# A ring of six one-chunk input buffers, and weights spaced for it, in a kernel of linear attention and soft mixture of experts

The kernel runs on one core of one Trainium2 chip. The metric is the device time of one execution in microseconds (us). A run is called slow when it lies over 1.5% above the fastest of the same kernel; only fast runs are compared. Expectations and captions call the changed kernel "after" and the original "before".

## What must be computed

The first half is a linear attention with a decaying state (4 batches, 8 heads, 768 steps, head size 48), the second a soft mixture of 8 experts with 4 slots each over all 3072 tokens of width 384.

```python
for t in range(S):                       # attention; r, k, v are [4, 8, 768, 48] float32
    cur = einsum('bhd,bhe->bhde', u * k[t], v[t])
    y[t] = einsum('bhd,bhde->bhe', r[t], state + cur)
    state = w * state + einsum('bhd,bhe->bhde', k[t], v[t])
x = y as [3072, 384]
logits = x @ phi                         # [3072, 32]
slots = softmax(logits, over tokens).T @ x
slot_out[e] = relu(slots[e] @ w1[e]) @ w2[e]   # w1 [8, 384, 1024], w2 [8, 1024, 384] float32
out = softmax(logits, over slots) @ slot_out   # [3072, 384]
```

No up-projection can start before the attention of all tokens is done, because the first softmax is over tokens.

## The kernel before

The attention works in 12 chunks of 256 steps, three to a batch. A chunk has 384 KB each of r, k and v. In SBUF one partition holds two neighbouring steps of a head, so a contiguous piece of a chunk, at both ends, is 2 x 48 floats, 384 bytes. Input copies are issued by SyncE and land in a pool of two batch-sized buffers. The first batch is loaded chunk by chunk, the other three with one copy for each of k, r and v.

```python
ld = ctx.enter_context(tc.tile_pool(name="ld", bufs=2))
SRC = ((1, k), (0, r), (2, v))

def load_part(bt, i):                    # first batch only: one chunk, 384 KB a copy
    for x, src in SRC:
        nc.sync.dma_start(out=bt[:, x, :, i, :],
                          in_=src[0, :, i * TS:(i + 1) * TS, :].rearrange("h (p j) d -> p h (j d)", j=J))

def load(b):                             # batches 1 to 3: three chunks, 1.18 MB a copy
    if b >= B:
        return
    bt = new_batch(b)
    for x, src in SRC:
        nc.sync.dma_start(out=bt[:, x].rearrange("p h i m -> p (h i) m"),
                          in_=src[b].rearrange("h (i p j) d -> p (h i) (j d)", p=P, j=J))
# ... cut ...
            if n % nSb == 1:             # in the loop over chunks: batch b+2 after chunk 1 of batch b
                load(n // nSb + 2)
```

GpSimd (POOL) issues the weights, which are cast from float32 to bf16 on the way, in between the three products it makes for each chunk. So a stalled product also delays the weights behind it.

```python
def w1_load(e):
    nc.gpsimd.dma_start(out=w1_all[:, e, :, :], in_=w1_ap[:, e, :, :])
# w_todo: w1 of experts 0 to 7, then w2 of experts 0 to 6, then w2 of expert 7 in four pieces
# experts 4 to 7 of w2 ("w_tail") lie in a batch buffer that has come free
W_IN = [0, 0, 1, 0, 0, 1, 1, 1, 1]       # weights issued inside mults(n + 3), by chunk n
W_AT = [0, 0, 1, 0, 0, 1, 1, 1, 3, 0, 0] # weights issued at the end of iteration n
# ... cut: load_w(2) before the loop ...

def mults(n, inner=0):                   # cut to chunks 1 to 11
    nc.gpsimd.tensor_mul(rr[:, :, :, 0:D], r_l, W_n[:])
    load_w(inner)
    nc.gpsimd.tensor_mul(kk[:, :, :, 0:D], k_l, W_k[:])
    nc.gpsimd.tensor_mul(ku, ku, u_b)
```

The rest of the attention takes from there: VectorE's `rkv` product (L283) needs POOL's last product, ScalarE's `v_bf` copy needs v. Then come the up-projection (`h_p`), two down-projections (`so_p`, `sr_p`), a scaled copy `so_r`, and the output.

The softmax here doesn't subtract the row's maximum and nothing guards it: scores larger than these inputs give would overflow.

## Time and profile before

| | before |
|---|---|
| median of the first 3 runs | 128.2 us (128.12 to 129.5) |
| span of the profiled execution | 126.4 us |
| up-projection starts on PE | 96.92 us |
| `so_r` starts | 108.83 us |
| moved by DMA in all | 31.78 MB |

Queue q0 holds what POOL issues, q1 what SyncE issues; the columns are packets, MB and share of the 16 engines' time.

```profile
DMA packets 23080, 31.78 MB, mean 251 GB/s; under 512 B 10451, under 2 KB 18005, under 8 KB 23061
...
q0 software_dynamic: 5360, 15.19, 56.7%
q1 hardware_dynamic: 17280, 16.32, 41.8%
```

The 36 chunk-sized pieces of input (3 tensors, 12 chunks) have 1024 rows of 384 bytes each, 36,864 rows in all. Yet q1 counts only 17,280 packets, and the output is among them. The nine copies of the first batch are 9 x 1024 = 9216 packets of 384 bytes; they make up most of the 10,451 "under 512 B". The other 18,005 - 10,451 = 7554 under 2 KB are mostly the nine batch-sized copies: each goes in 768 packets of 1536 bytes, four rows to a packet. The stretch from 15.91 to 20.50 us, in which only such copies moved, shows it directly: 983 packets, 1.48 MB, so 1506 bytes each.

### The profile page before, as it was taken

What the parts mean: (1) busy time and instruction counts of PE and PEld (TensorE: products, weight loads), DVE (VectorE), ACT (ScalarE), POOL (GpSimd) and SP (SyncE); (2) the same over time, 40 slices, a digit from 0 to 9 for tenths busy, and PEclk for the clock granted to TensorE, in tenths of its full rate; (3) what the DMA queues carried; (4) which work ended last, traced back from release to release, by engine and by line L of the source; (5) the groups of instructions that cost most, each with busy time, mean ns of one, the idle gap of its engine ahead of it and who ended that gap; (6) DMA issues with size and microseconds to landing.
All of it is one profiled execution on the core that took longest, in us unless ns stands there. A gap on an engine that the chain in (4) does not pass through costs nothing.

```text
span 126.4 us, 4165 instructions
## 1 busy us (share of the span) xinstructions
PE 97.5 (77%) x1783; PEld 70.5 (56%) x1783; DVE 91.7 (73%) x181; ACT 78.4 (62%) x144; POOL 81.4 (64%) x77
## 2 busy tenths in 40 slices
PE   3994898887599969189798969799999998793000
PEld 3493575665487757177576657677665565520000
DVE  5599989969989999578999798979762411497000
ACT  5869498868479968488597688886431510495000
POOL 6009999799999799999999999992420000055100
PEclk9999999999959999977999599958999999995555
DMA  3999998999999999999999999999999998079992
GB/s 84 299 325 325 335 327 264 321 208 251 265 332 267 235 259 270 340 289 270 258 255 252 226 211 223 221 214 215 210 218 212 218 199 160 2 264 372 381 403 81
DMA packets 23080, 31.78 MB, mean 251 GB/s; under 512 B 10451, under 2 KB 18005, under 8 KB 23061
## 3 DMA queue, kind: packets, MB, share of 16 engines
q0 software_dynamic: 5360, 15.19, 56.7%
q1 hardware_dynamic: 17280, 16.32, 41.8%
q8 instruction: 14, 0.23, 0.7%
q10 hardware_dynamic: 420, 0.00, 0.2%
q14 instruction: 6, 0.04, 0.1%
HBM read 39.38 MB, written 4.72 MB: 349 GB/s over the span
## 4 chain that ended last, share of the span: by engine, by line
POOL 33%; DMA 25%; PE 10%; SPq 9%; DVE 8%; issue 4%; ACT 2%; POOLq 1%; DVEq 0%
DMA w_tail<-in_moe_w_dram 16%; POOL kk L256 10%; POOL rkv L257 9%; DMA rkv<-in_r_dram 8%; SPq L75 7%; POOL rr L254 7%; DVE o_s L748 5%; POOL w_all L187 2%; POOL w_h L194 2%; PE t_p L312 2%; POOL hT L121 1%; SPq L83 1%; PE so_p L681 1%; PE sr_p L712 1%; PE aat_p L331 1%
## 5 line engine op out<-in xcount | busy, mean ns | idle before, releaser
L343 DVE TENSOR_TENSOR at_s<-aat_p,mask 128x512 bf16<-128x512 f32 x47 | 30.2, 684 | 4.0 <-PE aat_p L331 3.8
L254 POOL TENSOR_TENSOR rr<-rkv,W_n 128x768 bf16<-128x768 f32 x11 | 19.9, 1813 | 8.9 <-DMA rkv<-in_r_dram 8.7
L257 POOL TENSOR_TENSOR rkv<-rkv,u_rep 128x768 f32<-128x768 f32 x11 | 19.9, 1812 | 0.9
L256 POOL TENSOR_TENSOR kk<-rkv,W_k 128x768 bf16<-128x768 f32 x11 | 20.0, 1817 | 0.1
L331 PE MATMUL aat_p<-t_rr,t_kk 64*64 64x128 bf16 x376 | 12.1, 243 | 7.8 <-ACT t_kk L319 4.7
L277 ACT COPY rpun<-rkv 128x384 f32<-128x384 f32 x23 | 11.3, 490 | 10.3 <-PE rpun L491 8.2
L331 PEld LDWEIGHTS <-t_kk 64*64 64x64 bf16 x384 | 8.6, 119 | 11.2 <-ACT t_kk L319 6.9
L283 DVE TENSOR_TENSOR rkv<-rkv,rpun 128x384 f32<-128x384 f32 x23 | 12.6, 546 | 1.3 <-POOL rkv L257 1.1
L301 DVE TENSOR_TENSOR dv<-v_bf,rpun 128x768 bf16<-128x768 bf16 x12 | 11.4, 953 | 2.4 <-ACT v_bf L264 1.4
L319 ACT COPY t_kk<-t_p 128x1024 bf16<-128x1024 bf16 x12 | 12.2, 1014 | 1.0 <-PE t_p L312 1.0
L752 POOL DMA_DIRECT2D out_dram<-o_s x1 | 0.6, 552 | 18.4 <-ACT o_s L750 18.4
L294 DVE TENSOR_REDUCE rpun<-rkv 128x16 f32<-128x768 f32 x12 | 11.5, 961 | 0.4
L382 PE MATMUL s_p<-v_bf,kk 64*128 64x96 bf16 x160 | 11.8, 222 | 0.0
L319 ACT COPY t_rr<-t_p 128x1024 bf16<-128x1024 bf16 x11 | 11.2, 1016 | 0.5 <-PE t_p L312 0.3
L391 DVE TENSOR_TENSOR st<-s_p,wm 128x384 bf16<-128x384 f32 x20 | 10.9, 546 | 0.4 <-PE s_p L382 0.4
L264 ACT CAST v_bf<-rkv 128x768 bf16<-128x768 f32 x12 | 10.0, 830 | 1.8 <-DMA rkv<-in_v_dram 1.8
L382 PEld LDWEIGHTS <-kk 64*128 64x128 bf16 x160 | 8.5, 104 | 4.0 <-issue 3.9
L433 ACT COPY xt_s<-xl_p 128x768 bf16<-128x768 bf16 x11 | 8.8, 798 | 1.4 <-PE xl_p L431 1.1
L412 ACT CAST x_t<-y_p 128x384 bf16<-128x384 f32 x22 | 9.6, 495 | 0.0
L488 PE MATMUL rpun<-Lexp,x_t 128*128 128x32 bf16 x66 | 5.1, 179 | 5.2 <-DVE dv L301 5.2
L312 PE MATMUL t_p<-ident,kk 128*128 128x128 bf16 x96 | 8.8, 246 | 0.2 <-ACT t_rr L319 0.2
L312 PE MATMUL t_p<-ident,rr 128*128 128x128 bf16 x88 | 8.5, 253 | 0.0
(132 smaller groups left out, 194.7 us busy)
## 6 DMA issues: line engine op xcount, KB each, us to landing
w_all<-in_moe_w_dram POOLq DMA_DIRECT2D x8, 768.0 KB, 11.6
w_h<-in_moe_w_dram POOLq DMA_DIRECT2D x4, 768.0 KB, 13.2
w_tail<-in_moe_w_dram POOLq DMA_DIRECT2D x3, 768.0 KB, 19.7
out_dram<-o_s POOLq DMA_DIRECT2D x6, 384.0 KB, 6.7
out_dram<-o_s SPq DMA_DIRECT2D x5, 384.0 KB, 6.1
rkv<-in_k_dram SPq DMA_DIRECT2D x3, 384.0 KB, 4.4
rkv<-in_r_dram SPq DMA_DIRECT2D x3, 384.0 KB, 4.6
rkv<-in_v_dram SPq DMA_DIRECT2D x3, 384.0 KB, 5.3
```

What stands on the lines that cost most here:

```text
L254: nc.gpsimd.tensor_mul(rr[:, :, :, 0:D], r_l, W_n[:])
L256: nc.gpsimd.tensor_mul(kk[:, :, :, 0:D], k_l, W_k[:])
L257: nc.gpsimd.tensor_mul(ku, ku, u_b)
L277: nc.scalar.copy(rp, loads[n][0][:, j, :, :])
L283: nc.vector.tensor_mul(s["ku"][:, j, :, :], s["ku"][:, j, :, :], s["rps"][j])
L294: nc.vector.tensor_reduce(d, s["ku"], axis=mybir.AxisListType.X, op=ALU.add)
L301: nc.vector.tensor_mul(dv[:], s["v"][:], d[:, :, :, None].to_broadcast([P, J, H, D]))
L312: nc.tensor.transpose(t_p[:, q, :, j, :], s[nm][:, j, 2 * q:2 * q + 2, :].rearrange("p h d -> p (h d)"), ident[:])
L319: nc.scalar.copy(t_s[:], s.pop("p_" + nm)[:])
L331: nc.tensor.matmul(at_p[a][g * HF:(g + 1) * HF, q, :], kT[sl, q, g, j, :], rT[sl, q, g, :, :].rearrange("p j c -> p (j c)"), start=True, s ...
L343: nc.vector.tensor_mul(s["at"][:, a, j, :, :], at_p[a][:], mask[:, j, None, :].to_broadcast([P, nP, P]))
L382: nc.tensor.matmul(s_p[:, q * D2:(q + 1) * D2], s["kk"][sl, j, 2 * q:2 * q + 2, :].rearrange("p h d -> p (h d)"), s["v"][sl, j, 2 * q:2 * ...
```

## The change

The intent is a finer ring: a chunk's buffer comes free as soon as that chunk is done, so loads need not wait for a whole batch, and r comes first, because POOL's first product wants it. The bytes in SBUF are the same. The weights are spaced differently to leave room for the inputs. Experts 4 to 7 of w2 take one pair of chunk buffers each. SyncE sends both halves of the first output. The core of the diff:

```diff
-    ld = ctx.enter_context(tc.tile_pool(name="ld", bufs=2))
+    ld = ctx.enter_context(tc.tile_pool(name="ld", bufs=6))
-            nc.sync.dma_start(out=bt[:, x].rearrange("p h i m -> p (h i) m"),
-                              in_=src[b].rearrange("h (i p j) d -> p (h i) (j d)", p=P, j=J))
+        b, i = divmod(n, nSb)
+        bt = ld.tile([P, 3, H, J * D], f32, name="rkv")
+        for x, src in SRC if n == 0 else (SRC[1], SRC[0], SRC[2]):
+            nc.sync.dma_start(out=bt[:, x],
+                              in_=src[b, :, i * TS:(i + 1) * TS, :].rearrange("h (p j) d -> p h (j d)", j=J))
 ... load(0) .. load(5) at the start, then in the loop:
-            if n % nSb == 1:
-                load(n // nSb + 2)
+            load(n + 1 + NL)
 ... weights
-        W_IN = [0, 0, 1, 0, 0, 1, 1, 1, 1]
-        W_AT = [0, 0, 1, 0, 0, 1, 1, 1, 3, 0, 0]
+        W_IN = [0, 0, 1, 0, 1, 1, 1, 1, 1]
+        W_AT = [0, 0, 0, 0, 1, 1, 1, 1, 2, 0, 0]
-        load_w(2)
+        load_w(1)
 ... last expert of w2 in pieces of 4, 2, 2 columns instead of 2, 2, 2, 2; output
-            put = nc.sync.dma_start if i % 2 == 0 else nc.gpsimd.dma_start
+            put = nc.gpsimd.dma_start if i and i % 2 == 0 else nc.sync.dma_start
-                    (nc.sync if j == 0 else nc.gpsimd).dma_start(out=out_ap[i][:, j, :], in_=o_s[:, j, :])
+                    put(out=out_ap[i][:, j, :], in_=o_s[:, j, :])
```

More of the change, by code (lines that the diff above doesn't have):

```diff
@@ L57, with load @@
     w1_all = wts.tile([P, E, nM, F], bf, name="w1_all")
-    w2_h = [wts.tile([P, E // 2, nF, Dm], bf, name="w2_h")[:]]
+    w2_h = wts.tile([P, E // 2, nF, Dm], bf, name="w2_h")
+    w2_of = [w2_h[:, e] for e in range(E // 2)]
     ident = wts.tile([P, P], bf, name="ident")
-    ld = ctx.enter_context(tc.tile_pool(name="ld", bufs=2))
+    ld = ctx.enter_context(tc.tile_pool(name="ld", bufs=6))
     cst = ctx.enter_context(tc.tile_pool(name="cst", bufs=1))
     loads = {}
+    NL = 6
     SRC = ((1, k), (0, r), (2, v))
-    def new_batch(b):
-        bt = ld.tile([P, 3, H, nSb, J * D], f32, name="rkv")
-        for i in range(nSb):
-            loads[b * nSb + i] = [bt[:, x, :, i, :].rearrange("p h (j d) -> p j h d", j=J) for x in range(3)]
-        return bt
-    def load_part(bt, i):
-        for x, src in SRC:
-            nc.sync.dma_start(out=bt[:, x, :, i, :],
-                              in_=src[0, :, i * TS:(i + 1) * TS, :].rearrange("h (p j) d -> p h (j d)", j=J))
-    def load(b):
-        if b >= B:
-            return
-        bt = new_batch(b)
-        for x, src in SRC:
-            nc.sync.dma_start(out=bt[:, x].rearrange("p h i m -> p (h i) m"),
-                              in_=src[b].rearrange("h (i p j) d -> p (h i) (j d)", p=P, j=J))
-    b_first = new_batch(0)
-    load_part(b_first, 0)
+    def load(n):
+        if n >= nS:
+            return
+        b, i = divmod(n, nSb)
+        bt = ld.tile([P, 3, H, J * D], f32, name="rkv")
+        loads[n] = [bt[:, x].rearrange("p h (j d) -> p j h d", j=J) for x in range(3)]
+        for x, src in SRC if n == 0 else (SRC[1], SRC[0], SRC[2]):
+            nc.sync.dma_start(out=bt[:, x],
+                              in_=src[b, :, i * TS:(i + 1) * TS, :].rearrange("h (p j) d -> p h (j d)", j=J))
+    load(0)
     warm = cst.tile([P, 1], f32, name="warm")
@@ L101 @@
                             in_=w.rearrange("(q a) d -> a d q", a=2)[par])
-    for i in range(1, nSb):
-        load_part(b_first, i)
-    load(1)
+    for n in range(1, NL):
+        load(n)
     row_i = cst.tile([P, 1], mybir.dt.int32, name="row_i")
@@ L189, in w2_load @@
     def w2_load(e, f0=0, f1=nF):
-        if e == XE and f0 == 0:
-            tail = ld.tile([P, (E - XE) * nF * Dm], bf, name="w2_tail", tag="rkv",
-                           padded_shape=[P, 3 * H * nSb * 2 * J * D])
-            w2_h.append(tail[:].rearrange("p (e f d) -> p e f d", e=E - XE, f=nF))
-        nc.gpsimd.dma_start(out=w2_h[e // XE][:, e % XE, f0:f1, :], in_=w2_ap[:, e, f0:f1, :])
+        if e >= XE and f0 == 0:
+            tail = ld.tile([P, nF * Dm], bf, name="w2_tail", tag="rkv", padded_shape=[P, 2 * 3 * H * J * D])
+            w2_of.append(tail[:].rearrange("p (f d) -> p f d", f=nF))
+        nc.gpsimd.dma_start(out=w2_of[e][:, f0:f1, :], in_=w2_ap[:, e, f0:f1, :])
     w_todo = []
@@ L199 @@
     w_todo.pop()
-    for f in range(0, nF, 2):
-        w_todo.append((w2_load, (E - 1, f, f + 2)))
+    for f0, f1 in ((0, 4), (4, 6), (6, nF)):
+        w_todo.append((w2_load, (E - 1, f0, f1)))
     w_todo.reverse()
@@ L535 @@
         v_cast(0)
+        load(NL)
         tables()
@@ L681, in down @@
                     nc.tensor.matmul(so_p[c * ES:(c + 1) * ES, :], hT[:, x, fi, c * ES:(c + 1) * ES],
-                                     w2_h[x][:, c, fi, :],
+                                     w2_of[x * XE + c][:, fi, :],
                                      start=(x == 0 and fi == 0), stop=(x == 1 and fi == nF - 1),
@@ L712, in last_down @@
                     nc.tensor.matmul(sr_p[c][:], hL[:, fi, :, :].rearrange("p g t -> p (g t)"),
-                                     w2_h[1][:, XL, fi, c * HD:(c + 1) * HD],
+                                     w2_of[E - 1][:, fi, c * HD:(c + 1) * HD],
                                      start=(fi == 0), stop=(fi == nF - 1), skip_group_check=True)
-        last_down(0, 2)
         keep(2)
-        last_down(2, 4)
+        last_down(0, 4)
         keep(1)
```

## The prediction

> **What bounds the kernel now.** I read first the busy row by slices on the profile page, then the chain of work that ended last, then the waits, and last the engine-by-stretch table (us, then PE, PEld, DVE, ACT and POOL busy, clock, DMA share, GB/s).
>
> ```profile
> DVE  5599989969989999578999798979762411497000
> DMA  3999998999999999999999999999999998079992
> GB/s 84 299 325 325 335 327 264 321 208 251 265 332 267 235 259 270 340 289 270 258 255 252 226 211 223 221 214 215 210 218 212 218 199 160 2 264 372 381 403 81
> ```
>
> Two engines look full: VectorE until some 93 us, and the DMA engines from 3 to 107 us and again from 111 to 124. The GB/s row has two levels while the DMA row stays at 9: about 330 early (r, k, v, plain float32 copies) and about 214 later (weights, cast from float32 to bf16, so twice as much is read as is counted).
>
> ```profile
> 84.04 20.84 DMA w_tail<-in_moe_w_dram
> 104.88 0.04 issue
> 104.93 1.46 PE so_p L681 x22
> 106.39 0.44 PE sr_p L712 x4
> ...
> 108.46 0.34 PE sr_p L712 x4
> 108.80 0.02 issue
> 108.83 0.43 ACT so_r L727
> ```
>
> This is the chain, in order of time. The second down-projection stands until expert 6 of w2 lands at 104.88, 20.84 us after its issue: with the queue full, that is a place in a line and not a slow transfer. From there PE runs without a gap to 108.80, then the normalisation and the output follow. So this landing sets the end, and POOL, which the chain names for a third of the span, matters only in so far as it issues late.
>
> ```profile
> POOL rr L254 <- DMA rkv<-in_r_dram: 8.7, 3, 6.8
> ACT v_bf L264 <- DMA rkv<-in_v_dram: 1.8, 1, 1.8
> DVE dv L301 <- ACT v_bf L264: 1.4, 1, 1.4
> DVE rkv L283 <- POOL rkv L257: 1.1, 1, 1.1
> PE so_p L681 <- DMA w_tail<-in_moe_w_dram: 0.5, 1, 0.5
> ```
>
> These are rows of the waits (total us, times, longest). The batch-sized loads do hurt the attention: POOL waits three times for r, and VectorE loses 1.4 us to a late v and 1.1 us to a late product of POOL. But the last line shows how little that side leads or trails: PE comes to the landing only 0.5 us early, after six filler products (L689) that took 1.15 us.
>
> ```profile
> 14.00:20.00 6.00, 6.00 (x109) 4.60 (x108) 5.47 (x10) 5.07 (x9) 5.92 (x4) 1.00 1.09 330
> 20.50:22.00 1.50, 1.11 (x25) 0.74 (x24) 1.46 (x3) 1.45 (x3) 1.50 (x3) 1.00 0.69 200
> 25.50:28.50 3.00, 2.70 (x51) 2.08 (x50) 1.91 (x4) 2.05 (x3) 2.92 (x3) 1.00 1.11 209
> 54.00:55.00 1.00, 0.88 (x24) 0.71 (x24) 0.65 (x3) 0.83 (x3) 1.00 (x2) 1.00 0.80 190
> 72.00:104.00 32.00, 29.58 (x576) 21.02 (x574) 22.26 (x42) 17.69 (x36) 16.16 (x22) 0.94 1.06 214
> 106.00:107.50 1.50, 1.50 (x19) 0.99 (x13) 0.56 (x1) 0.00 (x0) 0.00 (x0) 1.00 0.58 102
> ```
>
> Here the DMA share is the next to last number: above 1 in full stretches, 0.69 and 0.80 in the two stretches where the queues ran thin, 0.58 where the last weights trickle in.
>
> **A budget for the DMA.** Inputs: 3 tensors x 12 chunks x 384 KB = 14.16 MB. At 330 GB/s that is 42.9 us (the first batch, in chunk pieces, ran at 325 from 6.5 to 13.5 us, which adds 0.2). Weights: 16 x 768 KB = 12.58 MB written, at 214 GB/s 58.8 us. Together 101.9 us. The DMA begins at about 2.3 us and the weights trickle out by 107, so 104.7 us are used and 2.8 us lost. What I can point to: start-up from 2.5 to 6.5 us at 297, 0.4 us; 20.5 to 22 us, share 0.69 against 1.09, 0.55 us; 54 to 55 us, 0.25 us; the trickle, 0.7 us; the remaining 0.9 us is spread over the mixed stretches. Whatever the change does to waits of POOL or VectorE, it can bring the last landing forward only out of these 2.8 us.
>
> **What the Trainium skill says.** (1) "DMA: Bandwidth & Descriptors", Queues, rings and completion order: each DMA engine goes round the queues packet by packet. The trace agrees: from 25.5 to 28.5 us the total is 209 GB/s, the weights' own rate, although SyncE had issued k of the third batch at 24.89; large weight packets crowd small input packets out. Weights sent early delay inputs, which is what spacing is for. (2) "HBM Reference", Specifications (TRN2): a core streaming alone reaches about 425 GB/s, bounded by its 16 engines. The weights' 214 GB/s written is 428 read, so that stretch has no more to give. (3) The DMA page, Rules for kernel authors, advises at least 1 MiB per DMA. The change cuts loads of 1.1 MB to 384 KB. The trace shows no such penalty with copies back to back: 325 against 330 GB/s. (4) Its Specifications put the first byte at about 1 us for copies issued by GpSimd and 0.6 us for SyncE. The trace agrees in direction: the first two output halves landed 2.5 us after SyncE's issue and 3.5 us after GpSimd's.
>
> **The change part by part.**
> Chunk ring. Removed: the batch-grained release, where chunks 6 to 8 could not start before chunk 2 was done (issue at 24.89). Added: 36 SyncE issues in place of 18, about 1.15 us each by the rows of the first batch, 41 us on an engine with nothing else to do. Chunks 6 and 7 can follow at once behind chunk 5, because chunks 0 and 1 are used up by 12 and 19 us. So the hole at 20.5 us closes: 0.55 us. Each x of a chunk is now contiguous in a partition, so I expect the first batch's packets to become like those of the later ones: 0.2 us at most.
> Order r, k, v. r of chunk 1 is sent second-tensor-first instead of after k, one copy of 384 KB earlier: about 1.2 us at 325 GB/s. POOL's 6.8 us wait shrinks to about 5.6. VectorE is not waiting for it there (its row has no gap before its first product of chunk 1), so nothing of it reaches the end.
> Spaced weights. One weight instead of two after the second chunk, two by the fifth chunk instead of four. POOL's step per chunk is 3 x 1.81 = 5.43 us plus 0.6 to 0.8 us per weight issue, so it runs from about 8.5 us to about 76 us, 3 to 4 us ahead of now. I checked that the DMA stays fed. From 24 us the queue holds chunks 6 and 7 (3.6 us each) and one weight (3.7 us), work until about 35; chunks 8 to 11 come free some 6.5 us apart and weights from 33 us on, faster than they drain, so a backlog of 4 us or more remains. No new hole, and the one at 54 us closes: 0.25 us.
> Attention. The stalls of 1.4 and 1.1 us go, so attention and the up-projection finish about 2.5 us earlier. But the second down-projection then waits some 3 us for expert 6 instead of 0.5: the landing still decides.
> w2 tail. The four buffers are free long before their issue at 75 to 80 us (chunk 9 is done one iteration earlier), so no wait. Three pieces of expert 7 instead of four save one POOL issue, 0.53 us, beside a full DMA queue: nothing. The same products and fillers follow; the first piece is now needed whole, which may cost 0.1 us.
> First output. Both halves from SyncE. The second half was issued by POOL at 111.02, and from 111.5 to 112.0 the DMA ran at only 89 GB/s; filling part of that saves about 0.2 us. The rest of the output runs at 383 GB/s and is not touched.
> Sum: 0.55 + 0.25 + 0.2 (packets) + 0.2 (output) - 0.1 = 1.1 us. 128.2 - 1.1 = **127.1 us**.
>
> **Rivals.**
> A: the attention chain is the true bound, and the end follows it by the whole 2.5 us, perhaps with an earlier first chunk: about 125.5. For it: PE arrives only 0.5 us before the landing. Against it: a 20.84 us landing and a full DMA row; weights cannot land faster than they are read.
> B: the spacing starves the DMA. If POOL falls behind, or SyncE stands on a ring buffer while few weights are queued, holes of 1 to 2 us appear between 30 and 60 us: about 129. For it: only two weights are queued by the fifth chunk. Against: the backlog worked out above.
> C: small input packets now compete with weights through the whole attention and arrive late, so VectorE's stalls move rather than go. The DMA total stays the same: about 128.
> D: mixing at chunk grain recovers the 0.9 us of unexplained loss as well: about 126.2.
>
> **Range and chances.** The middle is the budget; D and half of A give the low side, B and C the high side. Range 125.8 to 128.5. Over 2% faster means below 125.6, which needs nearly the whole 2.8 us; chance 0.14. Slower by over 2% means above 130.8, which needs a large new hole: 0.03. Within 2%: 0.83.
>
> **What would show it right or wrong.** Right: DMA at 9 without the hole at 20 us; POOL's total wait for r under 6.5 us; the waits of VectorE for v_bf and for POOL's product gone; attention ending some 2 to 3 us earlier; PE's wait for w_tail grown to 2 to 4 us; the last w_tail of 768 KB landing near 104; the first output near 109 us. Wrong: weights moving clearly faster than 214 GB/s, expert 6 landing before 102.5, or a DMA share under 0.9 in any stretch of 2 us between 6 and 104.

## The result

| | before | after |
|---|---|---|
| runs side by side | 128.12, 128.2, 129.5; slow: 132.33 | 135.55, 136.11; slow: 141.65, 151.54 |
| median of all four | 128.85 us | 138.88 us |
| ratio of fast runs, 95% interval | | 1.056 (1.045 to 1.068) |
| span of the profiled execution | 126.4 us | 134.3 us |
| up-projection starts | 96.92 us | 105.97 us |
| `so_r` starts | 108.83 us | 117.10 us |

A ratio here and below is the mean time of one kernel's fast runs over that of the other's fast runs of the same rounds, so it is not quite the ratio of the medians in the table. The kernel became 5.6% slower where 0.9% faster was expected.

The span grew by 7.9 us. By the three marks: the attention ends 105.97 - 96.92 = 9.05 us later; from there to `so_r` it takes 11.13 us instead of 11.91, 0.78 less; from `so_r` to the end 17.2 instead of 17.57, 0.37 less. So the whole loss lies in the attention, and the rest gave a little back.

POOL's and the DMA's busy rows by slices of 1/40 of the span (3.36 us), and the rate under them, after:

```profile
POOL 6049999999999999990840059999950000014100
DMA  3999999999999999999999999999999999049993
GB/s 89 303 325 325 325 293 236 201 286 246 245 205 295 255 245 215 238 215 207 211 212 214 225 259 267 218 230 214 215 212 212 221 206 180 10 164 349 379 397 124
```

The DMA engines are as full as before until the output. POOL is not: it stands around 62 us and from 68 to 79 us. The waits (us in all, times, longest) say for what:

```profile
POOL rr L244 <- DMA rkv<-in_r_dram: 15.7, 2, 10.1
...
DVE rkv L273 <- POOL rkv L247: 5.7, 2, 5.5
...
POOL kk L246 <- DMA rkv<-in_k_dram: 3.5, 1, 3.5
...
ACT v_bf L254 <- DMA rkv<-in_v_dram: 2.7, 1, 2.7
```

The 15.7 us are 5.6 for chunk 1, as predicted, and 10.07 for chunk 10; the 3.5 is for k of chunk 9. There is no row of PE waiting for `w_tail` any more, where before it stood 0.5 us. POOL's own timeline around it (start, us, and in brackets the idle time before and its releaser):

```profile
64.14 1.81 POOL L246 TENSOR_TENSOR kk<-rkv,W_k 128x768 bf16<-128x768 f32 x1 [3.50 <-DMA rkv<-in_k_dram]
...
78.65 1.80 POOL L244 TENSOR_TENSOR rr<-rkv,W_n 128x768 bf16<-128x768 f32 x1 [10.07 <-DMA rkv<-in_r_dram]
```

Until then POOL had been ahead of the kernel before (its second product of chunk 8 began at 53.59 instead of 55.42 us). After those two waits of 13.6 us its last product ends at 91.4 instead of 79.8 us. The chain that ended last (start, us, what) now leads through an input copy and not through a weight:

```profile
47.77 27.71 DMA rkv<-in_v_dram
...
105.97 2.77 PE h_p L642 x48
...
113.25 1.41 PE so_p L671 x24
...
117.10 0.43 ACT so_r L716
```

v of chunk 9 took 27.71 us from its issue to its landing. The bytes were no more than before, so I looked at the packets, over the whole execution:

```profile
DMA packets 44103, 31.79 MB, mean 237 GB/s; under 512 B 38370, under 2 KB 38884, under 8 KB 44084
...
q0 software_dynamic: 5072, 14.60, 52.4%
q1 hardware_dynamic: 38592, 16.91, 46.5%
```

All 36,864 rows of input are now packets of their own. No copy of a chunk, 384 KB in one block, gets the four-row packets that the batch-sized copies had. Then over the stretch from the landing of k of chunk 9 (64.1 us) to that of v of chunk 9 (75.5 us), which holds exactly one input copy:

```profile
q0 software_dynamic: 1008, 1.99, 92.2%
q1 hardware_dynamic: 1021, 0.39, 19.1%
```

This is the finding in two lines. **The two queues moved the same number of packets, 1008 and 1021**, but a weight packet brought some 1970 bytes (the mean; a row of w1 is 2048) and an input packet 384. The inputs got 0.39 MB in 11.4 us, 34 GB/s of a total of 212. In the kernel before, from 59.9 us to the landing of v of the fourth batch at 72.7 us, the same two queues moved:

```profile
q0 software_dynamic: 987, 1.95, 80.7%
q1 hardware_dynamic: 784, 1.18, 29.0%
```

There an input packet carried 1505 bytes: 1.18 MB in 12.8 us, 92 GB/s, from fewer packets. The stretch takes in both ends of the copy; in its middle, from 64 to 69 us, the count is one for one there too, 352 weight packets and 354 of inputs, with 0.70 and 0.54 MB. It is not so everywhere. Soon after weights begin to move, for one to three microseconds, the inputs got almost no packets, though copies had been issued: 11 beside 303 of weights from 25.5 to 28.5 us before the change, 5 beside 89 from 50 to 51 us after it. No run shows what holds them there.

What the inputs lost the weights did not gain: they moved 1.99 MB in 11.4 us after the change and 1.95 in 12.8 before, 175 against 152 GB/s, while the inputs fell from 92 to 34. Nor is it the clock, which was the same in these stretches (us, then PE, PEld, DVE, ACT and POOL busy, clock, DMA share, GB/s; first before, then after):

```profile
45.60:72.70 27.10, 21.74 (x454) 17.13 (x450) 23.15 (x39) 19.35 (x34) 26.54 (x18) 0.87 1.09 269
```

```profile
47.80:75.50 27.70, 23.01 (x491) 18.11 (x490) 23.70 (x40) 19.16 (x35) 16.99 (x13) 0.87 1.13 217
```

The clock is 0.87 in both. The rate fell from 269 to 217 GB/s at a DMA share of 1.09 and 1.13: the engines are as busy, but what they move is nearly all weights, for which twice the counted bytes are read. The landing times close the picture. Weights were issued at 45.7, 50.2, 52.8, 57.3, 59.8 and 67.8 us and landed at 55.0, 60.3, 64.8, 69.6, 73.7 and 78.2. Inputs that waited beside them landed at 64.1 (k of chunk 9) and 75.5 (v); then, when the weight queue ran dry at 78.2, r of chunk 10 landed at 78.6, k at 79.8, v at 81.0 and r of chunk 11 at 82.2, 1.2 us apart. The newer weights had overtaken the older inputs until none was left. SyncE was held up as well: to issue r of chunk 10 took it 10.74 us and k of chunk 10 another 11.27, against some 1.15 in the first batch, so that r of chunk 11 was not issued before 75.82 us. No run shows whether the input queue, slow as it was, held SyncE, or something else; from 56 to 75 us the inputs kept moving about one packet for each one of the weights.

### The profile page after: what moved, and what is told of

The parts are those of the page before. It is cut to its first block, busy times and chain, and to the rows that moved or that the text cites. A ratio compares the mean times of both kernels' runs of the same rounds, so it can differ in the third digit from the quotient of the medians.

```text
span 134.3 us, 4185 instructions
## 1 busy us (share of the span) xinstructions
PE 100.9 (75%) x1783; PEld 72.9 (54%) x1783; DVE 93.5 (70%) x181; ACT 78.7 (59%) x144; POOL 81.0 (60%) x74
## 4 chain that ended last, share of the span: by engine, by line
DMA 25%; POOL 21%; PE 19%; DVE 11%; SPq 10%; issue 5%; ACT 2%; POOLq 1%; DVEq 0%; ACTq 0%
DMA rkv<-in_v_dram 21%; SPq L76 10%; POOL kk L246 9%; POOL rr L244 6%; POOL rkv L247 4%; DVE o_s L737 4%; DMA rkv<-in_r_dram 4%; PE pad L507 2%; PE so_p L671 2%; PE h_p L642 2%; DVE at_s L333 2%; PE pad_f L679 1%; PE xl_p L421 1%; DVE rpun L284 1%; DVE dv L291 1%
## 5 line engine op out<-in xcount | busy, mean ns | idle before, releaser
L244 POOL TENSOR_TENSOR rr<-rkv,W_n 128x768 bf16<-128x768 f32 x11 | 20.4, 1854 | 15.8 <-DMA rkv<-in_r_dram 15.7
L246 POOL TENSOR_TENSOR kk<-rkv,W_k 128x768 bf16<-128x768 f32 x11 | 20.8, 1887 | 3.6 <-DMA rkv<-in_k_dram 3.5
L743 POOL DMA_DIRECT2D out_dram<-o_s x5 | 2.7, 547 | 22.7 <-DVE o_s L737 22.2
L291 DVE TENSOR_TENSOR dv<-v_bf,rpun 128x768 bf16<-128x768 bf16 x12 | 11.4, 954 | 3.0 <-ACT v_bf L254 2.0
L302 PE MATMUL t_p<-ident,rr 128*128 128x128 bf16 x88 | 9.4, 270 | 1.2 <-POOL rr L244 1.2
L302 PEld LDWEIGHTS <-rr 128*128 128x128 bf16 x96 | 8.4, 126 | 1.7 <-POOL rr L244 1.4
```

The lines of the kernel that those rows point to most:

```text
L291: nc.vector.tensor_mul(dv[:], s["v"][:], d[:, :, :, None].to_broadcast([P, J, H, D]))
L302: nc.tensor.transpose(t_p[:, q, :, j, :], s[nm][:, j, 2 * q:2 * q + 2, :].rearrange("p h d -> p (h d)"), ident[:])
```

## The experiments

**Theory P (packets).** An input cut to 384 KB goes in 384-byte packets, which get 384 / (384 + 2048) of the rate beside w1: with some 212 GB/s, 33.5 GB/s or 11.7 us a copy. This alone costs the time. **Rivals:** S, the new schedule of the weights does it; R, the ring itself does it (36 issues instead of 18, the order, buffers that come free late). All outputs of all runs were correct. Kernels are compared only within the same rounds.

### 1. The kernel before, with only the copies cut

```diff
 before:
-            nc.sync.dma_start(out=bt[:, x].rearrange("p h i m -> p (h i) m"), ...)
+            for i in range(nSb):
+                nc.sync.dma_start(out=bt[:, x, :, i, :],
+                                  in_=src[b, :, i * TS:(i + 1) * TS, :].rearrange("h (p j) d -> p h (j d)", j=J))
```

> The kernel before, with one thing changed: each load of a batch is cut in three along the chunks, so its packets are 384 bytes as in the changed kernel and not 1536; buffers, their release and the weight schedule stay. Packet theory (DMA engines go round the queues packet by packet, so 384-byte input packets get a small share beside weight packets of 2048 bytes written): the third batch (beside two to four weights) and the fourth (beside those from 54 us on) arrive late, v of the last chunks lands over 20 us after issue, VectorE and POOL wait several us more for them, 132 to 137 us. Schedule theory (the new spacing of the weights is at fault): no change, 128 to 129 us. Ring theory (waiting for a buffer chunk by chunk is at fault): no change, 128 to 129 us.

Measured: 135.38 and 135.78 in fast runs (two slow ones of 149.94 and 163.45), ratio **1.057 (1.053 to 1.060)**. The page's packet line and two rows of the waits, from the run of 135.78:

```profile
DMA packets 44103, 31.79 MB, mean 237 GB/s; under 512 B 38386, under 2 KB 39028, under 8 KB 44084
```

```profile
POOL rr L255 <- DMA rkv<-in_r_dram: 18.2, 2, 10.9
...
DVE rkv L284 <- POOL rkv L258: 5.8, 2, 5.5
```

The buffers, their release, the order and the weight schedule are those of before, so cutting the copies is enough to lose 5.7%. From 26 to 32 us the two queues again moved one packet each, 531 and 530. The granted clock was 0.89 here, and 0.86 to 0.91 in the fast runs of the kernel before, so the clock does not make the difference.

That the ratio is almost that of the change, 1.057 against 1.056, is in part luck, because the loss lies elsewhere. Here POOL stands for r of chunk 6 (10.95 us, until 51.4 us), not for chunks 9 and 10. The up-projection starts at 102.96 us, 6.04 later than before the change and not 9.05. From there to `so_r` it takes 13.41 us instead of 11.91, for the weights are late too: PE waits 1.5 us for `w_tail`. Whether the other parts help or hurt is the next question.

### 2 and 3. The weight schedule of one kernel in the other

Run 2 puts the old W_IN, W_AT and `load_w(2)` into the changed kernel, run 3 the new ones into the kernel before.

```diff
 run 2 (after); run 3 is the reverse, in before
-        W_IN = [0, 0, 1, 0, 1, 1, 1, 1, 1]
-        W_AT = [0, 0, 0, 0, 1, 1, 1, 1, 2, 0, 0]
-        load_w(1)
+        W_IN = [0, 0, 1, 0, 0, 1, 1, 1, 1]
+        W_AT = [0, 0, 1, 0, 0, 1, 1, 1, 3, 0, 0]
+        load_w(2)
```

> The changed kernel with the weight schedule of the kernel before (two weights after the second chunk, two by the fifth, none in iteration 4, three after iteration 8). Packet theory: weights in the queue while chunks 6 to 9 load now delay those, but fewer stand beside chunks 9 to 11, so part of the loss comes back: 130 to 135 us. Schedule theory: all of it comes back, 127 to 129 us. Ring theory: unchanged, 134 to 137 us.

> The kernel before with the new weight schedule alone, loads by the batch in 1536-byte packets. Packet theory: the large packets hold their share beside the weights of iterations 4 to 6, at most 1 to 3 us lost on the fourth batch: 127 to 131 us. Schedule theory: most of the loss appears, 133 to 137 us. Ring theory: 127 to 129 us.

Measured: run 2 had 138.74 to 140.4, all fast, ratio 1.086 (1.079 to 1.093). That is above all three expectations. POOL's wait for r was 21.3 us in five waits. Run 3 had 132.2, 133.44 and 134.05 fast, ratio 1.045 (1.039 to 1.051). Each schedule thus does better in its own kernel. In the changed kernel the new spacing is worth some 3% over the old one (1.086 against 1.056, each over its own runs of before), against my expectation that the old one would do better. In the kernel before, the new spacing does what rival B of the prediction feared. The busy row and the rate of run 3, slices of 3.26 us:

```profile
DMA  3999999999999669999999999999999998059992
GB/s 91 300 323 324 333 326 253 303 229 323 302 283 265 130 172 275 234 277 247 256 251 257 231 211 229 211 216 211 212 217 218 217 201 159 8 199 384 379 398 95
```

From 42 to 49 us the DMA thins to 130 and 172 GB/s: the batch ring cannot take the fourth batch before chunk 4 is done, and fewer weights are queued to fill the time. So S is a real cost for the batch ring, but not the cause of what the change lost.

Run 2 also says something of R. It has the small copies and the weight schedule of run 1, and beside them the ring, the order with r first, the new places of w2 and the output. It is some 3.8 us slower than run 1 (means of the fast runs, 139.4 and 135.6), and its up-projection starts at 109.06 us, 6.1 later. So something in these parts costs time beside the old weights, and the new spacing wins about as much back. No run takes these parts from each other; that their inputs only meet other weights is possible and not shown.

### 4. A second input queue

ScalarE instead of SyncE issues v of chunks 6 to 11, so these have a queue of their own, with turns of its own.

```diff
 after:
-            nc.sync.dma_start(out=bt[:, x],
+            (nc.scalar if x == 2 and n >= NL else nc.sync).dma_start(out=bt[:, x],
```

> The changed kernel with v of chunks 6 to 11 issued by ScalarE, so that the inputs stand in two queues beside the one of the weights. Packet theory: inputs get two turns in three while both queues hold something, about twice the bytes; k, r and v of chunks 9 and 10 land in about half of the 18 to 30 us they take now, and POOL's 10.1 us wait for r falls under 5 us; ScalarE pays six issues of 1 to 3 us; 128 to 133 us. Schedule and ring theories: no gain, 135 to 138 us.

Measured: 138.09 and 138.19 in fast runs, ratio 1.077 (1.074 to 1.079). The time I expected was missed. The profile fell in a slow run (142.73), so from it I read only what landed and waited in which order, and counts of packets, and explain no time by it. v of chunk 11, issued by ScalarE at 51.5 us, landed at 69.1. r of chunk 11, issued by SyncE at the same time, landed at 80.0 and k of chunk 11 at 94.7. The second queue did get turns of its own: from 56 to 66 us SyncE's queue moved 1116 packets and ScalarE's 973, beside 755 of weights. But v is not what POOL needs. With chunks 9 and 10 in time, POOL went on and issued more weights, and these then starved r and k of chunk 11, for which POOL waited 4.55 and 12.38 us. In that profile the loss had moved to the last chunk.

### 5 and 6. Weight packets of half the size, with a control

Run 5 loads each w1 in two halves of its columns, so that its rows and packets are 1024 bytes. Run 6 also makes two loads of each w1, but along the contraction, with rows of 2048 bytes as before.

```diff
 run 5 (after)
+        for fh in range(2):
+            fs = slice(fh * (F // 2), (fh + 1) * (F // 2))
+            nc.gpsimd.dma_start(out=w1_all[:, e, :, fs], in_=w1_ap[:, e, :, fs])
 run 6 (after)
+        for ms in (slice(0, 2), slice(2, nM)):
+            nc.gpsimd.dma_start(out=w1_all[:, e, ms, :], in_=w1_ap[:, e, ms, :])
```

> The changed kernel with each expert of w1 loaded in two halves of its columns, so that its packets are 1024 bytes written and not 2048; GpSimd pays one more issue (about 0.8 us) for each expert. Packet theory: an input packet of 384 bytes now meets 1024 and not 2048, so beside weights of w1 the inputs get 384 of 1408 bytes and not 384 of 2432, some 58 GB/s and not 33; k and v of chunk 9, 11.3 us apart at landing now, come about 7 us apart; POOL's waits for r and k after the first, 13.6 us now, fall to 6 us or less; against the next run (same issues, 2048 bytes) 2 to 6 us faster. Against the rest theory (only how many weights and when they are issued matters, not their packets): the same as the next run within 1 us.

> Control for the run before: the changed kernel with each expert of w1 in two loads too, but cut along the contraction, so packets stay 2048 bytes. Both theories: like the changed kernel, perhaps 1 to 2 us slower for GpSimd's eight more issues, 135 to 139 us, with POOL's waits for r and k at 10 us or more.

Measured: run 6, the control, had 136.08 and 136.61 fast, ratio 1.056 (1.048 to 1.064), as the changed kernel; POOL waited 10.99 us for r of chunk 10. Run 5 had 143.42 to 144.54 fast, ratio 1.115 (1.108 to 1.122). So the rate was predicted right and the time with the wrong sign. The queues of run 5 from the landing of v of chunk 9 at 63.4 us to that of k of chunk 10 at 78.2 us, with two input copies between:

```profile
q0 software_dynamic: 2238, 2.20, 87.6%
q1 hardware_dynamic: 2185, 0.82, 31.8%
```

Again one packet for one, 2238 and 2185, now with some 980 bytes in a weight packet. A copy took 14.8 / 2 = 7.4 us, against 11.4 with the 2048-byte rows; theory P said about 7 and 11.7. But POOL then stood at chunk 10 for only 4.52 us, for k. It issued two more loads, and the last chunk paid, in the POOL timeline of run 5:

```profile
93.63 1.79 POOL L246 TENSOR_TENSOR rr<-rkv,W_n 128x768 bf16<-128x768 f32 x1 [11.05 <-DMA rkv<-in_r_dram]
```

While POOL stood it issued no weights, and from 92.8 to 103.5 us (three slices) the DMA moved only 77 to 162 GB/s. In run 5, and in the slow profile of run 4, the partial cure moved the starvation to a later chunk and ended in an idle DMA. That this is why they are slower than the change is my reading, which no run tests by itself.

### 7. Weights spread evenly

```diff
 after:
-        W_IN = [0, 0, 1, 0, 1, 1, 1, 1, 1]
-        W_AT = [0, 0, 0, 0, 1, 1, 1, 1, 2, 0, 0]
+        W_IN = [0, 0, 0, 0, 0, 0, 0, 0, 0]
+        W_AT = [1, 1, 1, 1, 1, 1, 2, 2, 2, 0, 0]
```

> The changed kernel with the weights spaced evenly: one behind each of iterations 0 to 5, two behind 6 to 8, none inside a chunk's products. Packet theory: no burst of five weights in 14 us, so inputs get the whole DMA for some 3 us in each iteration of 6.5 us, which is a little under the 3.6 us that a chunk needs; waits of POOL for inputs shrink to 3 to 8 us but don't vanish; 129 to 134 us. If the ring itself (waiting for a buffer, chunk by chunk) costs the time: 134 to 138 us.

Measured: 141.19, 141.91 and 142.1 fast, ratio 1.098 (1.091 to 1.105). A clear miss. My reading, which no run tests by itself, is that some weights are then queued at all times, so that the inputs are never alone. The profile is of a slow run, and I draw nothing from it.

### 8. The output part alone

```diff
 before:
-            put = nc.sync.dma_start if i % 2 == 0 else nc.gpsimd.dma_start
+            put = nc.gpsimd.dma_start if i and i % 2 == 0 else nc.sync.dma_start
-                    (nc.sync if j == 0 else nc.gpsimd).dma_start(out=out_ap[i][:, j, :], in_=o_s[:, j, :])
+                    put(out=out_ap[i][:, j, :], in_=o_s[:, j, :])
```

> The kernel before with the output part of the change alone: both halves of the first output and the odd ones by SyncE, the even ones from the third on by GpSimd. All theories: 0.1 to 0.5 us faster than the kernel before, 127.7 to 128.3 us; the stretch from the last so_r to the end 17.2 us against 17.6.

Measured: 127.04 and 128.37 fast, ratio 0.989 (0.980 to 0.998). A small gain, within 2%.

### 9. The burst of weights held back

```diff
 after:
+        W_IN = [0, 0, 1, 0, 0, 0, 1, 1, 1]
+        W_AT = [0, 0, 0, 0, 0, 1, 2, 2, 2, 0, 0]
```

> The changed kernel with the burst of weights held back: one after the second chunk, one by the fifth, then none until iteration 5 is done, so two weights instead of seven are in the queue until GpSimd has issued the products of chunk 8 (about 56 us). Packet theory: inputs meet only two weights (7.4 us of weight time) before 56 us; chunks 9 to 11 land 15 us or more earlier than the 64 to 89 us of the changed kernel; POOL's waits for r and k after the first fall from 13.6 to under 4 us, attention ends near 95 us (105 now); the DMA now loses time in the middle instead, end at 128 to 132 us. If the ring (buffer by buffer) or the number of issues were at fault: waits of POOL and the time stay, 134 to 138 us.

Measured: one fast run of 135.01 and three slow ones from 143.28 to 155.45, so there is no ratio. The fast run is not near what I hoped for, and the profile is of a slow run. Inconclusive.

### 10. No weight before the eighth chunk

This takes the rival R apart from P: ring, issues and 384-byte packets stay, but no weight is in the way until 53.4 us, when all inputs have been issued.

```diff
 after:
-        W_IN = [0, 0, 1, 0, 1, 1, 1, 1, 1]
-        W_AT = [0, 0, 0, 0, 1, 1, 1, 1, 2, 0, 0]
-        load_w(1)
+        W_IN = [0, 0, 0, 0, 0, 0, 1, 1, 1]
+        W_AT = [0, 0, 0, 0, 0, 2, 2, 2, 2, 0, 0]
```

> The extreme of the run before: no weight at all before iteration 5 is done, so no stretch in which 384-byte input packets stand beside weights, except the last. Packet theory: POOL waits for r and k after the first for under 2 us, VectorE's waits for POOL and v vanish, attention ends at 92 to 94 us as its own work has it; inputs are done by about 50 us with holes in the DMA row between 24 and 50; all 59 us of weights come after that, so the last weight lands at 108 to 112 us and the time is 130 to 134 us, now by the DMA and not by attention. Ring theory: POOL still waits over 8 us, attention ends after 100 us.

Measured: 136.38 to 137.85, all fast, ratio 1.061 (1.054 to 1.068). About the time of the change, and above the 130 to 134 us that I expected, but for the opposite reason. Its rate by slices of 3.40 us and two rows of its waits:

```profile
GB/s 94 303 323 325 325 321 234 292 293 299 252 285 270 262 300 33 126 212 213 213 212 212 211 214 211 223 217 209 220 215 213 217 207 183 11 96 371 381 395 152
```

```profile
PE so_p L670 <- DMA w_tail<-in_moe_w_dram: 6.5, 2, 3.3
...
POOL rr L244 <- DMA rkv<-in_r_dram: 5.7, 1, 5.7
```

POOL waits for r only once, at the very start, and is done with the last chunk at 76.8 us, where the kernel before needs until 79.8 and the changed kernel until 91.4. VectorE no longer waits for POOL or v, and the up-projection starts at 95.79 us (96.92 before the change). So **the ring, its 36 issues and the 384-byte size do the attention no harm as long as no weight moves beside them**; R alone does not make the loss. What the ring adds beside weights (run 2) stays open. What costs here is the DMA: with inputs alone, issued as the ring's buffers come free, it moves 234 to 300 GB/s instead of 325 from 20 to 52 us, has a hole of some 4 us at 52 us, and then must bring all 12.58 MB of weights, the last of which lands at 116.5 us. The end hangs on that landing, as the prediction had thought of the changed kernel.

### 11. Large copies, r first

The kernel before with the two parts of the change that do not touch packets: the output of run 8, and r before k in batches 1 to 3.

```diff
 before, beside the output part of run 8:
-        for x, src in SRC:
+        for x, src in (SRC[1], SRC[0], SRC[2]):
```

> The kernel before with the output part of the change and with r ahead of k in the batches after the first: the parts of the change that don't touch the size of a load. POOL's later waits for r (0.9 and 1.1 us) go; the DMA line decides the end, so 127 to 128.3 us, 0.2 to 1 per cent faster than the kernel before. This is the candidate for a version that beats both.

Measured in five rounds: 127.11 to 128.77 fast, ratio 0.992 (0.985 to 0.999), the same within 2%. POOL's three waits for r became one, the first, of 6.8 us, and still the time barely moves: that wait time was beside the full DMA queue. Its interval overlaps with that of run 8, so r first has no gain that these runs can show. These two are the only versions that are not slower than the kernel before.

### 12 and 13. One batch at a time

These two came last, to see where in the attention the small packets hurt. Run 12 cuts only the second batch into chunk copies, run 13 only the third.

```diff
 before (b == 1 in run 12, b == 2 in run 13):
+            if b == 1:
+                for i in range(nSb):
+                    nc.sync.dma_start(out=bt[:, x, :, i, :],
+                                      in_=src[b, :, i * TS:(i + 1) * TS, :].rearrange("h (p j) d -> p h (j d)", j=J))
+                continue
```

> The kernel before with only the second batch (loaded at 10 to 27 us, for the most part before any weight is issued) in 384-byte pieces. If small packets cost only beside weights: 0 to 1.5 us slower, 128 to 130 us, all of it from the last of its pieces, which meet the first two weights after 20.6 us. If small packets cost by themselves: about a third of the loss of the run with all batches in pieces, 130.5 us or more.

> The kernel before with only the third batch (issued from 25 us on, while two weights, then two more, are in the queue) in 384-byte pieces. If small packets cost beside weights: most of the loss of the run with all batches in pieces, 133 to 136 us, and POOL waits for r of chunk 6 by 8 us or more (1.1 us before, 10.9 us with all in pieces). If by themselves: a third, about 130.5 us.

Measured: run 12 had 132.21, 132.57 and 133.37 fast, ratio 1.028 (1.018 to 1.037). By the terms set before the run this speaks for small packets that cost by themselves, against run 10. The run did not keep the two apart as it was meant to: by its profile, of a slow run, the last two copies of v were issued at 21.1 and 22.3 us, beside the first two weights at 21.2 and 22.0, and landed only at 36.3 and 37.5; from 27 to 31 us the queues moved 348 packets of weights and 351 of inputs. Run 13 had a single fast run of 133.18 (the kernel before: 128.62 to 129.92 fast), so no ratio, and POOL's wait at chunk 6, which I had expected to be 8 us or more, was 0.31 us; its 14.0 us for r were spread over five waits. So the sizes do not split by place as I thought. That what one batch loses shifts the next one against other weights is a guess. I take from these two only that the second batch alone in small packets, whose last copies stand beside weights, is enough to lose some 3%.

Over all runs theory P foretold rates and waits better than times. The rate of run 5 and POOL's free way in run 10 came as expected; the times of runs 2, 3, 4, 5, 7, 10 and 12 were all longer than P had them.

### What was not tried

The direct cure would be the six-buffer ring with four rows to a packet. No such kernel is among the runs, and none shows how a copy of 384 KB could get such packets. Whether the ring with large packets beats the kernel before stays open.

## Why the prediction was wrong

The call was "within 2%" with 0.83, and 127.1 us; it was 5.6% slower, outside the range. By its own steps:

- **The step that failed** is the sentence "Each x of a chunk is now contiguous in a partition, so I expect the first batch's packets to become like those of the later ones: 0.2 us at most." It was the other way round: the later batches became like the first, and packets under 512 bytes rose from 10,451 to 38,370. The page of the kernel before had the warning in one row: q1 counted 17,280 packets where 36,864 rows were to be moved, so something packed rows, and only the cut first batch was small. I had put the difference down to the layout in SBUF and had not asked what cutting the copy did. Run 1 settles it: the cut alone, with the old layout, makes the packets, and loses 5.7%. Whether it is the size of the copy or its 8 rows to a partition in place of 24, no run tells apart.
- **"The landing still decides"** fell with it. I treated the DMA as one line that serves in the order of issue, where an input can be late only by the backlog ahead of it. The backlog of weights was there as worked out, and the DMA row stayed full. But it is not ahead of the inputs, it is beside them, and takes 5 of 6 bytes. Attention ended 9.05 us later instead of 2.5 earlier, and PE did not wait for `w_tail` at all instead of some 3 us.
- **The point from the skill** about turns by packets was stated rightly and used for half of what it says. The prediction says "large weight packets crowd small input packets out", of the stretch from 25.5 to 28.5 us, where the inputs were still 1536 bytes. That stretch is no evidence of turns: 303 packets to 11 is not one for one. And the prediction did not ask what becomes of 384. The arithmetic was at hand: 384 / 2432 of 212 GB/s is 11.7 us for a copy, 11.4 measured.
- **The penalty of small copies** was judged by "325 against 330 GB/s", a measurement with nothing beside them. Alone, they are about as good: from 6.5 to 17 us they ran at 325 GB/s after the change and 324 in run 10, though at 293 in run 1. Beside large packets they had 34 GB/s.
- **Rival C** had the mechanism by name, "small input packets now compete with weights through the whole attention and arrive late", and the wrong size. It assumed that "the DMA total stays the same", so that only stalls would move. The total did stay near, but POOL issues the weights: when it stands for an input, later weights come later too.
- **Rival B** was right about the spacing and wrong about the ring: with the new spacing, holes appear with the batch ring (run 3) and not with the chunk ring.
- **Right, and small:** POOL's first wait for r went from 6.8 to 5.6 us as predicted. The hole at 20.5 us nearly closed (DMA share 0.96 instead of 0.69, at 251 GB/s). The part after `so_r` gained 0.37 us where 0.2 was expected. The 36 issues did the attention no harm where no weight moved beside them (run 10).
- **The signs** to watch were chosen to catch a missing DMA, "a DMA share under 0.9", or faster weights. Only the first fired, and only by its letter: 0.86 from 19.75 to 21.75 us, where the kernel before had its hole too, and from 78.25 to 80.25 us, after the long waits. Through the waits themselves the share was 1.13. The signs of being right did fail: POOL waited 15.7 us for r and not under 6.5, VectorE 5.7 us for POOL's product. A sign for a bandwidth that is full but goes to the wrong queue was missing: the rate of each queue, or the time of one copy from issue to landing.

What stays open: why the single input copies trail so far in the slow runs of 7 and 9; why kernels with small packets vary more (135 to 163 us in run 1, where before had 128 to 133); how much of run 12 is the packet's doing directly; what the ring, the order and the places of w2 cost beside weights (run 2 against run 1); and why the inputs get almost no packets just after weights begin.

## What to carry to other kernels

When a load is cut, compare the packets of the two queues and not only the bytes. Here two queues that both had work shared the engines packet for packet (352 to 354 with input packets of 1536 bytes, 1008 to 1021 with 384), so the one with small packets gets the small part, and its older copies are overtaken by newer ones of the other queue until that runs dry. Where the starved queue feeds the engine that issues the other, the loss can come back as idle DMA later (run 5). So keep a latency-critical load as coarse in its packets as it was (the kernel before lost nothing like this with 1536 bytes beside 2048; the ring with such packets was not run), or leave the bulk unissued until it has landed, and count what the delay of the bulk then costs (run 10).

## What the Trainium skill lacked or had wrong

- "DMA: Bandwidth & Descriptors", Queues, rings and completion order: it says that an engine goes round its queues packet by packet, and the runs agree almost to the packet where both queues have work (1008 to 1021, and 2238 to 2185), but not just after weights begin (303 to 11). It gives 9 to 17 descriptors as typical for a packet. Here each 384-byte row was counted as a packet of its own, and so the share of a queue could be 0.39 of 2.4 MB. The page does not draw the consequence that a queue's share goes by the size of its packets.
- No page says that a copy of 1.18 MB with rows of 384 bytes goes in packets of four rows and one of 384 KB with the same rows does not: 768 packets a copy (1506 bytes each in the trace) against 1024 for a third of the bytes.
- The same page, Rules for kernel authors: "≥1 MiB per DMA" holds here less for line rate than for the share beside another queue. Back to back, copies of 384 KB ran at 325 against 330 GB/s; beside weights at 34 against 92.
- The same page, Specifications, asks for at least 512 bytes for line rate. The 384-byte packets, alone, reached 325 GB/s before and after the change, and the 1536-byte ones 330, so there is hardly a loss there; run 1 had 293 for the same packets.
